# Another order of the parts of an attention step, and other last steps, in a fused attention and MoE kernel on one Trainium2 core

## The chip, the core and the metric

The kernel runs on one core of a Trainium2 chip. The core has a matrix engine (TensorE, PE in the rows; its weight loads are shown as PEld), a vector engine (DVE), an activation engine (ACT), GpSimd (POOL) and a sync engine (SP), which here issues all transfers. Each works through its own list of instructions in the order in which the program was written, and waits where an operand or a buffer is not ready. The metric is the time of one execution in microseconds, lower is better.

## What is computed

Causal attention over 2 batches of 12 heads (sequence 448, head size 64), then two blocks of matrix products over the 896 tokens, all in float32:

```python
scores = scale * np.matmul(q, k.transpose(0, 1, 3, 2))
scores = np.where(mask, -1000000000.0, scores)
scores = scores - np.max(scores, axis=-1, keepdims=True)
attn = np.exp(scores)
attn = attn / (np.sum(attn, axis=-1, keepdims=True) + 1e-09)
x = (attn @ v), heads side by side          # 896 x 768
h = np.maximum(np.maximum(x @ w1, x @ w2), x @ w3)      # 768 x 768 each
x = h @ w_out                                           # 768 x 768
h = x @ w_in                                            # 768 x 2048
r = np.maximum(h, 0.0)
out = (s * (r * r) + b) @ w_out2                        # 2048 x 768
```

## The kernel before

**Attention.** Two heads make a pair; 12 pairs are worked through in steps. `emit(p)` (line 434) writes the instructions of step p, for p from -1 to 13, by walking through one list of names, `ORDER` (line 28). One step holds parts of three pairs, and the list alone decides where each instruction stands on its engine. The names:

- `Sa` (of pair p+1), `Sb`, `Sc` (of pair p): scores on PE, of query tiles 1 and 0, of tile 2, of tile 3 (of 4 tiles of 112 rows). Each fills a PSUM tile `s`, of which there are two, so `Sb` needs the tile that `Sc` of the step before filled, `Sc` that of `Sa`, and the next `Sa` that of `Sb`.
- `Ra`, `Rb`, `Rc`: row maxima on DVE. `Ea`, `Eb`, `Ec`: exponentials on ACT, which read `s` and so set it free. (`Ra` belongs to the `Sa` that stands in the same step, `Ea` reads it in the next.)
- `TA0 TA1 TA2 TB0 TB1 TB2`: 20 transposes of the exponentials of pair p-1 on PE (A and B are the two heads) into three PSUM tiles `t`; `VA0` to `VB2`: their copies to SBUF (tile `PT`) on ACT.
- `N1 N2`: the row sums, 1e-9 added and inverted, on DVE. `RT`: their transpose on PE, which is written into the tile of `TB1`. `RV`: copy on DVE, `Q1`: store to DRAM on SP; one step later `Q2` reads it back spread over the partitions (tile `rb`).
- `PV`: the 16 products with v of pair p-2 on PE. `XM`: divided (times `rb`) on DVE, `XO` and `XL`: split into a high and a low part of x on POOL.
- `LD`: loads on SP of pair p+3; `QS`, `HS`, `LS`: scaling (POOL), high part (DVE) and low part (POOL) of q and k of pair p+2.

**Weights.** Each weight tile (128 x 768, 8-byte words, 768 KB) comes by `fetch_w` and is taken apart in two halves, "chunks", by `decode` (line 137): two passes on ACT, three on DVE (`second` and `third` are put off to `finish`, name `Y` in the list), one addition on POOL (`rounded`, one chunk later), a copy of the high part on ACT, a subtraction of the low part on DVE (`split`, two chunks later). `W1`, `W2`, `W3` each begin a chunk; `CHUNKS` says in which steps. The third weight tile can only be fetched once the second chunk has been read, since there are two raw tiles.

**Early products.** Two of the products of the first MoE block need only batch 0, whose pairs are done half way through. `early_products` (line 521) is a generator over 12 pieces of three matmuls, and `M` in the list (`EARLY`, line 36) takes six of them in step 12 and six in step 13. The product of the first weight tile leaves PSUM by a copy on ACT that stands at the head of the generator's second half.

**MoE.** `moe()` then runs 1404 and 672 matmuls back to back on PE, with one chunk per product.

Of the kernel before, what the change touches and what calls it, by code (L numbers as in the profile page):

```python
# [8 lines left out]
F32 = mybir.dt.float32  # L9
# [6 lines left out]
ALU = mybir.AluOpType  # L16
# [7 lines left out]

ORDER = (
    "Q2 LD TA0 TA1 TA2 Ea N1 N2 Sb Rb VA0 VA1 VA2 Y W1 Sc Eb Rc Y QS PV XM HS XO LS XL "
    "TB0 VB0 TB1 VB1 RT RV Q1 Y W2 TB2 VB2 M Y Sa Y W3 Ra Ec Y"  # L30
).split()


FETCH = 9
CHUNKS = {10: "W3", 11: "W2", 12: "W1 W2 W3", 13: "W1 W2"}
EARLY = {12: 6, 13: 6}
MASKED = -(2.0 ** 30)
OVER = 122880.0
UNDER = 2.0 ** -15
# [9 lines left out]
def kernel(  # L49
# [36 lines left out]
    ident = const.tile([128, 128], F32, name="ident")  # L86
    sb = const.tile([128, 2], F32, name="sb")
    ones = const.tile([128, 512], mybir.dt.bfloat16, name="ones")

    def sub_lo(eng, lo, full, hi):  # L90
        eng.tensor_tensor(out=lo, in0=full, in1=hi.bitcast(F32), op=ALU.subtract)  # L91
# [45 lines left out]
    def decode():  # L137
        if not raws:
            return
        c = n_chunk[0] % 2  # L140
        mine = []
        n_chunk[0] += 1
        raw = raws.pop(0) if c else raws[0]
        words = raw.bitcast(I32).rearrange("p (n t) -> p n t", t=2)
        cs = slice(c * HW, (c + 1) * HW)
        a = wa_p.tile([128, HW], I32, tag="wa", name="wa")
        r = wd_p.tile([128, HW], I32, tag="wr", name="wr")
        f = a.bitcast(F32)
        low, high = (words[:, cs, n] for n in range(2))
        fhigh = raw.bitcast(F32).rearrange("p (n t) -> p n t", t=2)[:, cs, 1]  # L150
        nc.scalar.activation(out=r, in_=low.bitcast(U32), func=ACTF.Copy, scale=2.0 ** -29)  # L151
        nc.scalar.activation(out=f, in_=fhigh, func=ACTF.Abs)  # L152
        nc.vector.tensor_scalar(  # L153
            out=f, in0=f, scalar1=UNDER, scalar2=OVER, op0=ALU.max, op1=ALU.min
        )

        def second():
            nc.vector.tensor_scalar(  # L158
                out=a, in0=a, scalar1=3, scalar2=0x3FFFFFF8,
                op0=ALU.logical_shift_left, op1=ALU.bitwise_and,  # L160
            )

        def third():
            nc.vector.scalar_tensor_tensor(  # L164
                out=a, in0=high, scalar=-0x40000000, in1=a,
                op0=ALU.bitwise_and, op1=ALU.bitwise_or,
            )
            if c:
                fetch_w()

        def rounded():
            nc.gpsimd.tensor_tensor(out=a, in0=a, in1=r, op=ALU.add)  # L172
            if c == 0:
                tiles["w"] = (
                    w_p.tile([128, DM], F32R, tag="whi", name="whi"),
                    w_p.tile([128, DM], F32R, tag="wlo", name="wlo"),
                )
            mine.extend(tiles["w"])
            hi = mine[0]
            rest.append(lambda: nc.scalar.copy(out=hi[:, cs], in_=f))  # L180

        def split():
            hi, lo = mine
            sub_lo(nc.vector, lo[:, cs], f, hi[:, cs])
            if c:
# [14 lines left out]
    def attention():  # L200
        with ExitStack() as c2:
# [104 lines left out]

                return maxima, exponentials

            def pool_copy(out, in_):
                nc.gpsimd.tensor_scalar(  # L310
                    out=out, in0=in_, scalar1=1.0, scalar2=1.0, op0=ALU.mult, op1=ALU.mult
                )

            def weights_out(p, ps):

                e = pair[p]
# [55 lines left out]

            def pv_out(p):
                b, kx = p // NP, p % NP
                e = pair[p]
                x = n_p.tile([128, S], F32, tag="xf", name="xf")
                hi, lo = (xt[kx][:, n, b * S:(b + 1) * S] for n in range(2))

                def divide():
                    nc.vector.tensor_tensor(  # L380
                        out=x, in0=e["o"][:, 0:S], in1=e["rb"], op=ALU.mult
                    )

                def high():
                    pool_copy(hi, x)

                def low():
                    sub_lo(nc.gpsimd, lo, x, hi)

                return divide, high, low  # L390

# [42 lines left out]
            def emit(p):  # L434
# [18 lines left out]
                if 0 <= p - 1 < n_pairs:  # L453
                    d = {}
                    for h, k in enumerate("AB"):
                        for n, js in (("0", (0,)), ("1", (1,)), ("2", (2, 3))):
                            ops["T" + k + n] = lambda n=k + n, h=h, js=js: d.update(
                                {n: transpose_p(p - 1, h, js)}
                            )
                            ops["V" + k + n] = lambda n=k + n: nc.scalar.copy(  # L460
                                out=d[n][0], in_=d[n][1]
                            )
                    su = pair[p - 1]["su"]
# [11 lines left out]
                    ops["Q1"] = lambda: pair[p - 1]["r"][2]()  # L475
                if 0 <= p - 2 < n_pairs:
                    ops["Q2"] = lambda: pair[p - 2]["r"][3]()
                    ops["PV"] = lambda: pv(p - 2, (0, 1, 2, 3))
                    for n, fn in zip(("XM", "XO", "XL"), pv_out(p - 2)):
                        ops[n] = fn  # L480
                if p in EARLY:
                    ops["M"] = lambda: [next(first, None) for _ in range(EARLY[p])]
# [3 lines left out]
                for n in ORDER:  # L486
# [10 lines left out]
            for _ in first:  # L497
                pass


    t_p = ctx.enter_context(tc.tile_pool(name="tmp", bufs=4))
    early = {}
# [18 lines left out]
    def early_products(pool, tag):  # L521
# [164 lines left out]
```

## Time and profile before

| | |
|---|---|
| time, median of 3 runs | 551.66 us (549.05 to 557.89) |
| time of the profiled execution | 549.17 us |
| its span, first to last instruction | 547.4 us |
| busy: PE, PEld, DVE, ACT, POOL | 94%, 84%, 61%, 56%, 43% |
| first MoE matmul of the unbroken stream | at 142.46 us |

Busy shares are means over a kernel of two different halves: up to 142 us attention, then a stream of matmuls. Times in the rows are microseconds from the span's start. A matmul's end is modelled, so where one group of matmuls stops is better read from the start of the next instruction on PE.

### The profile page before, as it was taken

The page shows a single profiled execution, that of the slowest core. Times are in us where ns is not written, and L with a number is a line of the kernel's source. Part 1 is how long each engine was busy: PE and PEld are TensorE (multiplying, and loading weights), DVE is VectorE, ACT ScalarE, POOL GpSimd, SP SyncE. Part 2 cuts the span into 40 slices and gives each one's busy share as a digit, 9 for nine tenths or more (in the row PEclk, how much of TensorE's full clock was granted, in tenths as well). Part 3 has the DMA queues.
Part 4 walks back from the last instruction along what each step waited for, and adds up shares of the span by engine and source line. Part 5 has one row for each costly group of instructions (what it writes and reads, how often), then busy time and mean ns, then how long its engine had stood idle before and what let it go on. Part 6 is the DMA issues. An engine that isn't in the chain of part 4 may idle for free.

```text
span 547.4 us, 8432 instructions
## 1 busy us (share of the span) xinstructions
PE 517.3 (94%) x3094; PEld 461.0 (84%) x3094; DVE 331.7 (61%) x637; ACT 308.6 (56%) x743; POOL 233.0 (43%) x218
## 2 busy tenths in 40 slices
PE   8988878876999999999999999999999999999997
PEld 4656565645899999999999999999999999999997
DVE  3456565547565756566566666676778875567601
ACT  3577776765344534535455478888888743344301
POOL 4336364324343534434433346655665633324200
PEclk9999999978899999999999999999999999999999
DMA  7042422422333223333232233333222353253102
GB/s 235 18 136 74 130 83 72 147 79 76 116 105 127 73 101 122 110 117 117 106 115 90 102 108 117 115 116 115 92 90 109 115 173 112 89 187 121 57 1 101
DMA packets 16185, 58.39 MB, mean 107 GB/s; under 512 B 2384, under 2 KB 6224, under 8 KB 16144
## 3 DMA queue, kind: packets, MB, share of 16 engines
q1 hardware_dynamic: 16144, 57.85, 32.0%
q8 instruction: 24, 0.39, 0.3%
q14 instruction: 17, 0.14, 0.1%
HBM read 55.05 MB, written 2.80 MB: 106 GB/s over the span
## 4 chain that ended last, share of the span: by engine, by line
PE 89%; ACT 6%; DVE 2%; DMA 1%; POOL 1%; issue 1%; ACTq 0%; DVEq 0%; POOLq 0%
PE m L510 53%; PE m L619 21%; PE o L365 4%; PE s L277 4%; ACT P L301 3%; PE t L350 2%; ACT PT L460 2%; PE warm L423 2%; DVE mx L293 2%; DMA wraw<-in_w_dram 1%; PE s L284 1%; PE warm L395 1%; PE t L323 1%; POOL wa L172 0%; ACT wr L151 0%
## 5 line engine op out<-in xcount | busy, mean ns | idle before, releaser
L510 PE MATMUL m<-x,whi 128*128 128x448 f32 x816 | 234.0, 368 | 4.6 <-ACT t L519 3.8
L172 POOL TENSOR_TENSOR wa<-wa,wr 128x384 int32<-128x384 int32 x112 | 129.3, 1154 | 215.7 <-DVE wa L164 185.1
L510 PEld LDWEIGHTS m<-x,whi 128*128 128x128 f32 x816 | 154.6, 190 | 17.5 <-ACT t L519 4.0
L510 PE MATMUL m<-x,wlo 128*128 128x448 f32 x408 | 150.1, 368 | 0.0
L153 DVE TENSOR_SCALAR wa<-wa 128x384 f32<-128x384 f32 x112 | 71.1, 635 | 82.4 <-ACT wa L152 82.4
L619 PE MATMUL m<-whi,g 128*128 128x384 f32 x448 | 113.8, 334 | 0.0
L180 ACT CAST whi<-wa 128x384 fp32r<-128x384 f32 x112 | 56.9, 509 | 79.0 <-PE m L619 36.7
L510 PEld LDWEIGHTS m<-x,wlo 128*128 128x128 f32 x408 | 77.4, 190 | 6.2
L619 PEld LDWEIGHTS m<-whi,g 128*128 128x128 f32 x448 | 81.0, 188 | 0.0
L91 DVE TENSOR_TENSOR wlo<-wa,whi 128x384 fp32r<-128x384 f32 x112 | 62.6, 560 | 23.5 <-ACT whi L180 23.5
L619 PE MATMUL m<-wlo,g 128*128 128x384 f32 x224 | 74.8, 334 | 0.0
L164 DVE SCALAR_TENSOR_TENSOR wa<-wraw,wa 128x384 int32<-128x384 int32 x112 | 62.8, 560 | 3.9
L151 ACT ACTIVATE wr<-wraw 128x384 int32<-128x384 uint32 x112 | 61.4, 549 | 0.2 <-DMA wraw<-in_w_dram 0.2
L152 ACT ACTIVATE wa<-wraw 128x384 f32<-128x384 f32 x112 | 60.6, 541 | 0.0
L301 ACT ACTIVATE P<-s,mx 112x224 f32<-112x224 f32 (+3 forms) x96 | 46.8, 502 | 14.1 <-DVE mx L293 13.7
L293 DVE TENSOR_REDUCE mx<-s 112x2 f32<-112x448 f32 (+3 forms) x48 | 34.0, 731 | 27.4 <-PE s L284 27.3
L158 DVE TENSOR_SCALAR wa<-wa 128x384 int32<-128x384 int32 x112 | 42.8, 382 | 3.8
L460 ACT COPY PT<-t 112x336 f32<-112x336 f32 (+1 forms) x72 | 30.6, 484 | 25.2 <-PE t L350 25.0
L619 PEld LDWEIGHTS m<-wlo,g 128*128 128x128 f32 x224 | 42.0, 188 | 0.0
L510 PE MATMUL m<-h,whi 128*128 128x448 f32 x144 | 40.9, 365 | 0.0
L277 PE MATMUL s<-HL 64*112 64x224 f32 (+3 forms) x288 | 31.3, 331 | 8.3 <-ACT P L301 8.3
L91 POOL TENSOR_TENSOR g<-r,g 128x448 fp32r<-128x448 f32 x32 | 37.2, 1163 | 0.0
(55 smaller groups left out, 485.5 us busy)
## 6 DMA issues: line engine op xcount, KB each, us to landing
wraw<-in_w_dram SPq DMA_DIRECT2D x56, 768.0 KB
R<-in_qk_dram SPq DMA_DIRECT2D x11, 448.0 KB
V<-in_v_dram SPq DMA_DIRECT2D x12, 224.0 KB
rb<-rcd SPq DMA_DIRECT2D x24, 112.0 KB
out_dram<-o SPq DMA_DIRECT2D x14, 192.0 KB
R<-in_qk_dram SPq DMA_DIRECT2D x2, 224.0 KB
rcd<-rows SPq DMA_DIRECT2D x12, 3.5 KB
sb<-in_s_dram SPq DMA_DIRECT2D x1, 0.5 KB
```

The lines of the kernel that those rows point to most:

```text
L91: eng.tensor_tensor(out=lo, in0=full, in1=hi.bitcast(F32), op=ALU.subtract)
L151: nc.scalar.activation(out=r, in_=low.bitcast(U32), func=ACTF.Copy, scale=2.0 ** -29)
L152: nc.scalar.activation(out=f, in_=fhigh, func=ACTF.Abs)
L153: nc.vector.tensor_scalar(out=f, in0=f, scalar1=UNDER, scalar2=OVER, op0=ALU.max, op1=ALU.min)
L164: nc.vector.scalar_tensor_tensor(out=a, in0=high, scalar=-0x40000000, in1=a, op0=ALU.bitwise_and, op1=ALU.bitwise_or,)
L172: nc.gpsimd.tensor_tensor(out=a, in0=a, in1=r, op=ALU.add)
L180: rest.append(lambda: nc.scalar.copy(out=hi[:, cs], in_=f))
L277: nc.tensor.matmul(ps[:, h, o:o + n], hl[h][:, a, qs], hl[h][:, c, 0:n], start=(m == 0), stop=False, skip_group_check=True,)
L293: nc.vector.tensor_reduce(out=e["mx"][:, i], in_=ps[:, :, o:o + n], op=ALU.max, axis=mybir.AxisListType.X, negate=True,)
L301: nc.scalar.activation(out=e["P"][:, h, poff[i]:poff[i] + n], in_=ps[:, h, o:o + n], func=ACTF.Exp, bias=e["mx"][:, i, h:h + 1], scale=1.0 ...
L510: nc.tensor.matmul(p, wt[w][:, ws], cols(act[i], a, b), start=(i == 0 and n == 0), stop=(i == len(act) - 1 and n == 2),)
L619: nc.tensor.matmul(acc[t][:, 0:EH], gt[f][:, a, ts], w[:, ws], start=(f == 0 and n == 0), stop=(f == KG - 1 and n == 2),)
```

## The change

- `ORDER` is replaced: within a step the scores `Sc` and `Sa` now come after all 20 transposes, the product with v is last on PE (split in four names `P0` to `P3`, of two to six instructions that are the same as before), and `RT` stands ahead of the copies `VB0`, `VB1` instead of behind them.
- Steps 12 and 13 have lists of their own, `ORDER_END`. Step 13 holds the product with v of the last pair, then both early products, `M1` and `M2`, each with the copy (or maximum) that takes it out of PSUM right behind its matmuls.
- Chunks: one in step 10, one in step 11, two in step 12, three in step 13 (before one, one, three, two). They start at another place of the step.
- The first two chunks are "light": the absolute value is taken on DVE (`bitwise_and`) instead of ACT, and the high part of the first of them is copied on POOL instead of ACT.
- Step 12 takes `VA1` and `VB1` on DVE. The last two pairs take the high part of x on ACT, the last also its low part on DVE. The last pair's product with v goes to an `s` tile, so that it need not wait for the only `o` tile.

```diff
-EARLY = {12: 6, 13: 6}
-CHUNKS = {10: "W3", 11: "W2", 12: "W1 W2 W3", 13: "W1 W2"}
+CHUNKS = {10: "W1", 11: "W1", 12: "W1 W2", 13: "W1 W2 W3"}
+LIGHT = 2
...
-    "Q2 LD TA0 TA1 TA2 Ea N1 N2 Sb Rb VA0 VA1 VA2 Y W1 Sc Eb Rc Y QS PV XM HS XO LS XL "
+    "TA0 Q2 LD Ea TA1 QS VA0 Sb TA2 VA1 VA2 Rb N1 N2 W1 HS TB0 TB1 RT Eb RV Q1 Y TB2 Sc Sa "
+    "P0 Rc VB0 VB1 Ra Y VB2 P1 P2 P3 LS XM XO XL Ec"
...
+    "P0 P1 P2 P3 Q2 W1 M1 Y Y W2 XM XO XL M2 Y Y W3 Y Y".split(),
...
-        nc.scalar.activation(out=f, in_=fhigh, func=ACTF.Abs)
+        light = n_chunk[0] <= LIGHT
+        if light:
+            nc.vector.tensor_scalar(
+                out=a, in0=high, scalar1=0x7FFFFFFF, scalar2=None, op0=ALU.bitwise_and
+            )
+        else:
+            nc.scalar.activation(out=f, in_=fhigh, func=ACTF.Abs)
...
-            rest.append(lambda: nc.scalar.copy(out=hi[:, cs], in_=f))
+            if light and c == 0:
+                pool_copy(hi[:, cs], f)
+            else:
+                rest.append(lambda: nc.scalar.copy(out=hi[:, cs], in_=f))
...
-                    e["o"] = ps_o.tile([128, 512], F32, tag="o", name="o")
+                    if p == n_pairs - 1:
+                        e["o"] = ps_s.tile([128, 2, 512], F32, tag="s", name="o")[:, 0]
+                    else:
+                        e["o"] = ps_o.tile([128, 512], F32, tag="o", name="o")
...
             for i in range(KD):
                 terms(p[:, m], early["w"][m], xt, 0, i)
-                yield
             evacuate_max(p[:, m], early["t"], m)
+            yield
```

On PE, one step in the middle of attention (s are scores, with the causal mask added by further rows that are left out; t transposes; o the product with v; the lone `t<-ident,su` is `RT`). Before:

```order
L350 MATMUL t<-ident,P 112x112 x10
L277 MATMUL s<-HL 112x336 x6
...
L277 MATMUL s<-HL 112x448 x6
...
L365 MATMUL o<-PT,V 64x448 x2
...
L350 MATMUL t<-ident,P 112x112 x7
L323 MATMUL t<-ident,su 8x112
L350 MATMUL t<-ident,P 112x112 x3
L277 MATMUL s<-HL 112x224 x6
```

and with the change:

```order
L364 MATMUL t<-ident,P 112x112 x7
L296 MATMUL s<-HL 112x336 x6
...
L364 MATMUL t<-ident,P 112x112 x10
L337 MATMUL t<-ident,su 8x112
L364 MATMUL t<-ident,P 112x112 x3
L296 MATMUL s<-HL 112x448 x6
...
L296 MATMUL s<-HL 112x224 x6
...
L382 MATMUL o<-PT,V 64x448 x2
```

The product with v moved from the middle of the step, between the scores of tile 3 and the second head's transposes, to its end, behind the next pair's first scores.

On DVE, the same step (mx are the maxima, `su` the row sums `N1` and `N2`, xf is `XM`, HL is `HS`, rows is `RV`). Before, from `Ra` on, and with the change, from `Rb` on:

```order
L293 TENSOR_REDUCE mx<-s 112x2 x2
L464 TENSOR_SCALAR su<-su 112x8
L467 RECIPROCAL su<-su 112x8
L293 TENSOR_REDUCE mx<-s 112x2 x2
L380 TENSOR_TENSOR xf<-o,rb 128x448
L239 CAST HL<-R 128x2x448
L326 COPY rows<-t 8x112
```

```order
L312 TENSOR_REDUCE mx<-s 112x2
L487 TENSOR_SCALAR su<-su 112x8
L490 RECIPROCAL su<-su 112x8
L258 CAST HL<-R 128x2x448
L340 COPY rows<-t 8x112
L312 TENSOR_REDUCE mx<-s 112x2 x3
L397 TENSOR_TENSOR xf<-o,rb 128x448
```

The two row-sum instructions now stand behind `Rb`, and `XM` is the last of a step, ahead of the next step's `Rb`.

On ACT, the end of attention up to the copy that takes the first early product out of PSUM (wr and wa are the two passes of a chunk over its raw tile, whi its high part). Before, and with the change:

```order
L151 ACTIVATE wr<-wraw 128x384
L152 ACTIVATE wa<-wraw 128x384
L180 CAST whi<-wa 128x384
L151 ACTIVATE wr<-wraw 128x384
L152 ACTIVATE wa<-wraw 128x384
L519 COPY t<-m 128x448
```

```order
L161 ACTIVATE wr<-wraw 128x384
L168 ACTIVATE wa<-wraw 128x384
L199 CAST whi<-wa 128x384
L161 ACTIVATE wr<-wraw 128x384
L168 ACTIVATE wa<-wraw 128x384
L540 COPY t<-m 128x448
```

The rows read alike. The last chunk ahead of the copy is the fifth in both, the first half of the third weight tile; what moved is the matmuls: before, PE has 16 products with v of the last pair between the two early products, with the change both early products follow each other.

## Rows read from the trace of the kernel before

**Rows 1.** Stretches: busy us (instructions) of PE, PEld, DVE, ACT, POOL; PEclk, DMA share, GB/s.
```profile
40.00:60.00 20.00, 16.14 (x173) 11.74 (x169) 11.53 (x20) 13.58 (x47) 9.84 (x9) 1.00 0.29 97
119.00:121.00 2.00, 2.00 (x7) 0.77 (x8) 0.40 (x2) 1.81 (x5) 0.00 (x0) 0.50 0.95 381
```
**Rows 2.** Waits of PE from 25 to 104 us: us in total, times, longest.
```profile
PE s L277 <- ACT P L301: 8.3, 9, 0.9
PE t L323 <- ACT PT L460: 6.1, 9, 0.7
```
**Rows 3.** Timeline of one step: start us, us, engine, line, operation, tiles, count [idle before].
```profile
60.01 0.26 PE L323 MATMUL t<-ident,su 112*8 112x112 f32 x1 [0.68 <-ACT PT L460]
...
60.49 0.56 PE L277 MATMUL s<-HL 64*112 64x224 f32 x6
...
61.48 1.17 PE L350 MATMUL t<-ident,P 112*112 112x112 f32 x10
...
61.59 0.92 DVE L293 TENSOR_REDUCE mx<-s 112x2 f32<-112x448 f32 x2 [1.02 <-PE s L284]
...
62.15 1.14 POOL L91 TENSOR_TENSOR x<-xf,x 128x448 fp32r<-128x448 f32 x1
62.43 0.89 DVE L464 TENSOR_SCALAR su<-su 112x8 f32<-112x8 f32 x1
...
62.58 0.72 PE L277 MATMUL s<-HL 64*112 64x336 f32 x6
...
63.26 0.56 POOL L233 TENSOR_SCALAR R<-R 128x448 f32<-128x448 f32 x1
...
63.47 0.83 DVE L293 TENSOR_REDUCE mx<-s 112x2 f32<-112x672 f32 x1
...
64.32 0.86 PE L277 MATMUL s<-HL 64*112 64x448 f32 x6 [0.92 <-ACT P L301]
...
65.22 2.11 PE L365 MATMUL o<-PT,V 112*64 112x448 f32 x16
...
65.33 1.09 DVE L293 TENSOR_REDUCE mx<-s 112x2 f32<-112x896 f32 x1 [1.03 <-PE s L284]
...
67.25 0.88 PE L350 MATMUL t<-ident,P 112*112 112x112 f32 x7
67.37 0.62 DVE L380 TENSOR_TENSOR xf<-o,rb 128x448 f32<-128x448 f32 x1 [0.95 <-PE o L365]
```
**Rows 4.** Timeline: the first transposes of step 2 and of step 11.
```profile
26.26 1.17 PE L350 MATMUL t<-ident,P 112*112 112x112 f32 x10
...
105.49 0.50 PE L350 MATMUL t<-ident,P 112*112 112x112 f32 x3
```
**Rows 5.** Chain that ended last: start us, us, what (62 us: one step; then the end).
```profile
62.63 1.65 ACT P L301 x8
...
67.89 0.88 ACT PT L460 x2
...
135.05 6.64 PE m L510 x18
...
142.46 284.81 PE m L510 x1404
```
**Rows 6.** Waits of PE from 104 to 143 us.
```profile
PE m L510 <- ACT t L519: 3.8, 1, 3.8
PE t L350 <- ACT P L301: 3.2, 2, 2.6
```
**Rows 7.** Timeline: fetches of weight tiles, and the divisions whose rb stood behind them.
```profile
96.12 1.17 SPq L134 DMA_DIRECT2D wraw<-in_w_dram  x2
...
105.19 0.62 DVE L380 TENSOR_TENSOR xf<-o,rb 128x448 f32<-128x448 f32 x1 [3.56 <-PE s L284]
...
129.09 0.36 SPq L134 DMA_DIRECT2D wraw<-in_w_dram  x1
...
134.52 0.62 DVE L380 TENSOR_TENSOR xf<-o,rb 128x448 f32<-128x448 f32 x1 [1.43 <-DMA rb<-rcd]
```

More of the change, by code (lines that the diff above doesn't have):

```diff
@@ L28 @@
 ORDER = (
-    "Q2 LD TA0 TA1 TA2 Ea N1 N2 Sb Rb VA0 VA1 VA2 Y W1 Sc Eb Rc Y QS PV XM HS XO LS XL "
-    "TB0 VB0 TB1 VB1 RT RV Q1 Y W2 TB2 VB2 M Y Sa Y W3 Ra Ec Y"
+    "TA0 Q2 LD Ea TA1 QS VA0 Sb TA2 VA1 VA2 Rb N1 N2 W1 HS TB0 TB1 RT Eb RV Q1 Y TB2 Sc Sa "
+    "P0 Rc VB0 VB1 Ra Y VB2 P1 P2 P3 LS XM XO XL Ec"
 ).split()
+ORDER_END = (
+    "TA0 VA0 TA1 VA1 TA2 VA2 Q2 N1 N2 TB0 VB0 TB1 RT VB1 RV Q1 TB2 VB2 W1 P0 P1 P2 P3 Y Y "
+    "XM XO XL W2 Y Y".split(),
+    "P0 P1 P2 P3 Q2 W1 M1 Y Y W2 XM XO XL M2 Y Y W3 Y Y".split(),
+)
 FETCH = 9
-CHUNKS = {10: "W3", 11: "W2", 12: "W1 W2 W3", 13: "W1 W2"}
-EARLY = {12: 6, 13: 6}
+CHUNKS = {10: "W1", 11: "W1", 12: "W1 W2", 13: "W1 W2 W3"}
+LIGHT = 2
 MASKED = -(2.0 ** 30)
@@ L88, with pool_copy @@
     ones = const.tile([128, 512], mybir.dt.bfloat16, name="ones")
+    def pool_copy(out, in_):
+        nc.gpsimd.tensor_scalar(
+            out=out, in0=in_, scalar1=1.0, scalar2=1.0, op0=ALU.mult, op1=ALU.mult
+        )
     def sub_lo(eng, lo, full, hi):
@@ L151, in decode @@
         nc.scalar.activation(out=r, in_=low.bitcast(U32), func=ACTF.Copy, scale=2.0 ** -29)
-        nc.scalar.activation(out=f, in_=fhigh, func=ACTF.Abs)
+        light = n_chunk[0] <= LIGHT
+        if light:
+            nc.vector.tensor_scalar(
+                out=a, in0=high, scalar1=0x7FFFFFFF, scalar2=None, op0=ALU.bitwise_and
+            )
+        else:
+            nc.scalar.activation(out=f, in_=fhigh, func=ACTF.Abs)
         nc.vector.tensor_scalar(
@@ L307, in scores @@
                 return maxima, exponentials
[L309 to L312, printed above, removed]
             def weights_out(p, ps):
@@ L384, in high @@
                 def high():
-                    pool_copy(hi, x)
+                    if p < n_pairs - 2:
+                        pool_copy(hi, x)
+                    else:
+                        nc.scalar.copy(out=hi, in_=x)
                 def low():
-                    sub_lo(nc.gpsimd, lo, x, hi)
+                    sub_lo(nc.gpsimd if p < n_pairs - 1 else nc.vector, lo, x, hi)
                 return divide, high, low
@@ L459, in emit @@
                             )
-                            ops["V" + k + n] = lambda n=k + n: nc.scalar.copy(
+                            copy = nc.scalar.copy
+                            if p == n_pairs and n == "1":
+                                copy = nc.vector.tensor_copy
+                            ops["V" + k + n] = lambda n=k + n, copy=copy: copy(
                                 out=d[n][0], in_=d[n][1]
@@ L477, in emit @@
                     ops["Q2"] = lambda: pair[p - 2]["r"][3]()
-                    ops["PV"] = lambda: pv(p - 2, (0, 1, 2, 3))
+                    for j in range(NC):
+                        ops[f"P{j}"] = lambda j=j: pv(p - 2, (j,))
                     for n, fn in zip(("XM", "XO", "XL"), pv_out(p - 2)):
                         ops[n] = fn
-                if p in EARLY:
-                    ops["M"] = lambda: [next(first, None) for _ in range(EARLY[p])]
+                if p == n_pairs + 1:
+                    ops["M1"] = ops["M2"] = lambda: next(first)
                 for n in CHUNKS.get(p, "").split():
@@ L485, in emit @@
                 ops["Y"] = lambda: finish(1)
-                for n in ORDER:
+                for n in ORDER if p < n_pairs else ORDER_END[p - n_pairs]:
                     if n in ops:
@@ L496, in attention @@
                     fetch_w()
-            for _ in first:
-                pass
     t_p = ctx.enter_context(tc.tile_pool(name="tmp", bufs=4))
```

## The prediction

> **What bounds the kernel now.** I first read the stretches, for where PE is not the bound. From 142.46 us on PE runs 1404 matmuls in 284.81 us without a gap, 0.203 us each [rows 5]; the change touches nothing there but the first chunks, so what can be won lies ahead of 142.46. In the middle of attention PE is busy 16.14 of 20 us, ACT 13.58, DVE 11.53, POOL 9.84 [rows 1]: no engine is full, so it is the order that costs. The waits say which: nine times PE waits some 0.92 us before scores, for exponentials, and nine times some 0.68 us before the row-sum transpose, for a copy [rows 2]. Nine steps, from step 2's first transposes to step 11's, take 105.49 - 26.26 = 79.23 us, 8.80 each [rows 4].
>
> The timeline of one step gives PE's work, from the start of one group to that of the next [rows 3]: `RT` with three transposes 0.48 (60.01 to 60.49); `Sa` 0.99 (to 61.48); ten transposes 1.10 (to 62.58), so 0.11 each; `Sb` 0.82 (64.32 less the wait of 0.92, less 62.58); `Sc` 0.90 (64.32 to 65.22); the product with v 2.03 (to 67.25); seven transposes 0.77 at 0.11. That is 7.09 of work, 1.60 of waits, and 0.11 left over. Why `Sc` waits: it takes the PSUM tile of `Sa`, which is last in a step, so maxima (0.92) and exponentials (1.65 in all) [rows 3, 5] have only ten transposes and `Sb` to hide under. Why `RT` waits: it writes into the tile that `VB1` still copies.
>
> **The steady step, part by part.** `Sa` now precedes the product with v, so its maxima and exponentials have 2.03 us more cover, and `Sc` comes after all transposes: the 0.92 goes. `RT` stands ahead of `VB1`: the 0.68 goes. Matmuls and their sizes are the same. What is late next? `RT` needs the inverted sums, `N1` and `N2`, and these now stand behind `Rb` on DVE. I walk one step from its first transposes at 0. `TA0`, `TA1` take 0.77, `Sb` ends at 1.59, `Rb` starts 0.11 later (as 61.59 follows 61.48) and ends at 2.53 with its 0.83 [rows 3]. On PE three and seven transposes reach 2.69. On POOL: the product with v ended at 0, `XM` starts 0.12 after it (67.37 to 67.25) and takes 0.62, to 0.74; `XO` some 0.56 by the like `QS`, to 1.4 with its start; `XL` 1.14, to 2.6. In the row of before `N1`, 8 elements wide, lasts 0.89, and it ends at 63.32, just as `XL` does (62.15 + 1.14 = 63.29) [rows 3]: it is held by POOL. So here it ends at about 2.64, `N2` fits in 0.15 (63.32 to 63.47), and `RT` starts at 2.85: a wait of 0.16. Then 0.48, 0.90, 0.99 and 2.03 to 7.25.
>
> The Trainium skill, page "SBUF — State Buffer", section "Who interferes with whom", says that DVE and GpSimd share one port pair, as a lock that whoever issues first holds for its whole instruction. The trace agrees with the lock (0.89 us for `N1`).
>
> The rest fits in 7.25: `Rc` from 4.34 to 5.43, `Ra` behind it to 6.4, `Ec` after `Rc` at most 1.65, to 7.1, before `Sb` of the next step at 8.0; `Ea` from 7.1 to 8.8, two copies at 0.44 [rows 5] to 9.7, which is 2.4 into the next step, where `TB1` needs the second from 2.3 on: even with this upper bound, 0.1. `HS` waits for `QS` until about 3.2, `RV` and `VB1` are behind it, and nothing on PE needs them before the next step. `rb` is asked for at the start of a step and read at its end. With the same 0.11 over, a step is 7.09 + 0.16 + 0.11 = **7.36**, 1.44 less than 8.80; nine give **13.0**. Step 1 has the wait for `VB1` too, so some **0.7** more; its warm-up matmuls stay.
>
> **Chunks in steps 10 and 11.** Two raw tiles are fetched behind step 9's `Q1`, some 4.5 us into that step. Before, tiles and `rb` of 96.12 were in at 105.19 at the latest [rows 7], 9.1 later; here that is 6.2 us into step 10, and `XM`, now last, asks at 7.4. So the late `XM` of step 10 goes, without time of its own. The light chunk moves a pass from ACT to DVE. Nothing of before shows this `bitwise_and`; I bound it by `N2`'s 0.15 and, behind a POOL instruction, by `XL`'s 1.14, and take 0.5, nearest to `XM`, a DVE pass over 448 columns in 0.62 where this one has 384. In step 10 three such passes and `RV` meet a gap of 1.5 us between `N2` and `Rc`; `Rc` is 0.3 late at most, and `Ec` still ends with the product with v. In step 11 POOL's addition and copy of chunk 1 stand beside chunk 2, and I let `Rc` and so `Ec` come 0.6 late.
>
> **The end**, from step 11's first transposes: 36.97 us before (142.46 - 105.49). Now step 11 has no `Sa`: 7.36 - 0.99 = 6.4. Step 12 has 20 transposes and `RT`, 2.3 of work; `Ec` is 0.6 late, and the wait for copies and for `N1` behind `XL` I set at 0.7, between nothing and the 2.6 that such a wait for exponentials lasted before [rows 6]: to 10.0. A stretch of transposes with holes is where the clock fell before: behind the wait of 2.6, from 119 to 121, the granted clock was 0.50 [rows 1], the 1.2 GHz level, and after a wait of 3.8 us the 18 matmuls from 135.05 took 6.64 instead of 18 x 0.203 = 3.65, 1.82 times as long [rows 5, 6]. I let one product with v run so: 3.7, to 13.7. The other 2.0, to 15.7. First early product 3.65, to 19.4; its copy out of PSUM 0.8 (as 141.69 to 142.46 before [rows 5]), to 20.2; second 3.65, to 23.8; 0.8 again, **24.6**. That is 36.97 - 24.6 = **12.4** less.
>
> What must hide under it: `XM` of pair 10 needs `rb` behind the third weight tile, which is fetched at about 6.7 (after chunk 2's last pass) and was in 134.52 - 129.09 = 5.4 later with `rb` [rows 7]: 12.1, against 13.7. ACT reaches the third tile at about 16 and finds it there; before, PE stood 3.8 us for the copy behind it [rows 6]. Taking copies to DVE and x's high part to ACT at the end costs nothing as long as that holds; else each is one 0.44 or 0.62 on the path.
>
> **Sum.** 0.7 + 13.0 + 12.4 = 26.1, off the profiled execution's 549.17 (its span 547.4, and 1.8 around it): **523.1 us**. That execution is 2.5 below the median of the runs shown and next to their lowest, so I take it as the typical one and leave 2.5 of room above.
>
> **Rivals.**
> - *POOL holds `N1` longer.* `QS` follows `XL` on POOL without a gap; if it is taken first, `N1` ends 0.56 later [rows 3]. For it: `N1` waits right at that seam. Against: in the row `N1` was out at 63.32 though `QS` stood ready at 63.26. Nine times 0.56: 528.1. By the Trainium skill's rule that whoever issues first holds the lock, this is what an earlier `QS` would do.
> - *The clock holds at the end.* Waits in step 12 are short. 1.7 less: 521.4.
> - *A weight comes late in steps 12 and 13*: the chain of ACT, DVE and POOL per chunk outlasts the matmuls. As long as the wait of before, 3.8 [rows 6]: 526.9.
> - *The steps don't get shorter*: `XM`, now ahead of the next `Rb` on DVE, waits for `rb`, `Rb` and `RT` follow. It needs `rb` 1.44 us behind the product with v in each step. Against: `rb` is asked for a step earlier, and only fetches of 768 KB held it. Then only the end is won: 536.8.
> - *Slower*: the clock falls in the steady steps, where PE now does transposes and scores for 5 us before the product with v. At 1.82 times, 7.09 becomes 12.9, 5.8 more per step; the forecast's gain is gone from the fifth such step on (26.1 / 5.8 = 4.5), nine give 575. Against: from 40 to 60 the clock was 1.00 with longer waits than are left [rows 1].
>
> **Chances.** Forecast 0.51 (519 to 527 by itself), held `N1` 0.14, clock holds 0.13, late weight 0.13, steps as long 0.05, clock falls 0.04. The range reaches from the case without clock loss and without the wait of 0.16 (some 518) to held `N1` with 2.5 of spread above, 531. Within 2% of 551.66, 540.6 to 562.7, is about what a measurement of this kernel can't tell from no change; only a few slow-clock steps end there or above: faster 0.94, same 0.03, slower 0.03.
>
> **What would show it.** First transposes of neighbouring steps 7.2 to 7.5 us apart; no wait of PE for exponentials before `Sc`, none for a copy before `RT`, but a short one for DVE's reciprocal; `N1` ending with `XL`. The first unbroken MoE matmul at 116 us. A step of 7.9 means that `QS` holds `N1`; 8.8 that the step is bound elsewhere; a granted clock of 0.50 outside step 12, or a wait of over 2 us in the early products, makes the end wrong.

## The result, and the profile after

The changed kernel takes 523.73 us (median of 4 runs, 523.55 to 526.89) against 550.66 us before (4 runs, 549.05 to 557.89): a ratio of 0.953, 95% interval 0.948 to 0.959. The profiled execution took 523.55 us, its span is 521.6 us, against 549.17 and 547.4. The forecast was 523.1 with a range of 518 to 531. The total is right; two of its terms are not, in opposite directions.

In the changed kernel line numbers are 10 to 23 higher: L364 is a transpose of exponentials, L337 the transpose of the sums (`RT`), L296 and L303 scores, L382 the product with v, L312 maxima, L320 exponentials, L483 their copies, L487 and L490 `N1` and `N2`, L397 `XM`, L96 and L101 the copy (`XO`) and the subtraction (`XL`) that split x, L405 the same copy on ACT, L531 a product of the first MoE block, L540 and L538 the copy and the maximum that take it out of PSUM. I read three pieces in it, as in the prediction: from the start of the program to the first transposes of step 2 (the head), nine steps from there to step 11's, and the end, from there to the unbroken stream.

**The steps.** Waits of PE in the changed kernel from 24 to 91 us (us in total, times, longest), which answer to [rows 2]:

```profile
PE t L337 <- DVE su L490: 1.7, 8, 0.2
PE t L364 <- ACT PT L483: 1.2, 1, 1.2
```

The two waits that came nine times before, 0.9 for exponentials and 0.7 for a copy, are gone. What is left is the announced short wait for the reciprocal, and one wait of 1.2 us that nobody announced. One step in the timeline of the changed kernel (start, us, engine, line, operation, tiles, count [idle before]), against [rows 3]:

```profile
57.90 0.89 PE L364 MATMUL t<-ident,P 112*112 112x112 f32 x7
...
58.02 0.62 DVE L397 TENSOR_TENSOR xf<-o,rb 128x448 f32<-128x448 f32 x1 [0.98 <-PE o L382]
...
59.38 1.14 POOL L101 TENSOR_TENSOR x<-xf,x 128x448 fp32r<-128x448 f32 x1
...
59.46 1.17 PE L364 MATMUL t<-ident,P 112*112 112x112 f32 x10
59.58 0.86 DVE L312 TENSOR_REDUCE mx<-s 112x2 f32<-112x672 f32 x1 [0.94 <-PE s L303]
60.35 0.19 DVE L487 TENSOR_SCALAR su<-su 112x8 f32<-112x8 f32 x1
...
60.58 0.20 DVE L490 RECIPROCAL su<-su 112x8 f32<-112x8 f32 x1
...
60.84 0.26 PE L337 MATMUL t<-ident,su 112*8 112x112 f32 x1 [0.20 <-DVE su L490]
...
61.32 0.86 PE L296 MATMUL s<-HL 64*112 64x448 f32 x6
...
62.09 0.55 PE L296 MATMUL s<-HL 64*112 64x224 f32 x6
...
63.07 2.11 PE L382 MATMUL o<-PT,V 112*64 112x448 f32 x16
...
65.11 0.88 PE L364 MATMUL t<-ident,P 112*112 112x112 f32 x7
```

`Sc` (61.32), `Sa` (62.09) and the product with v (63.07) follow each other without a gap, and a step lasts 65.11 - 57.90 = 7.21 us, against 8.80. PE is busy 19.58 of 20 us in this stretch, against 16.14 [rows 1]:

```profile
40.00:60.00 20.00, 19.58 (x223) 14.69 (x220) 12.26 (x25) 17.39 (x61) 11.96 (x11) 1.00 0.39 116
...
103.00:107.00 4.00, 4.00 (x33) 2.20 (x33) 3.29 (x8) 2.28 (x6) 0.97 (x2) 1.00 0.43 144
```

**The end.** The second of these stretches (columns as in [rows 1]) is that of the last two products with v, at a granted clock of 1.00, the 2.4 GHz level; before, a stretch at this place had 0.50 [rows 1]. The timeline of the end:

```profile
93.98 0.88 PE L364 MATMUL t<-ident,P 112*112 112x112 f32 x7
...
100.33 1.18 PE L364 MATMUL t<-ident,P 112*112 112x112 f32 x10
101.67 0.88 PE L364 MATMUL t<-ident,P 112*112 112x112 f32 x7 [0.15 <-ACT PT L483]
...
102.87 4.00 PE L382 MATMUL o<-PT,V 112*64 112x448 f32 x32
106.79 0.67 PE L531 MATMUL m<-x,whi 128*128 128x448 f32 x2
...
111.38 0.67 PE L531 MATMUL m<-x,whi 128*128 128x448 f32 x2 [0.67 <-ACT t L540]
...
115.53 0.63 DVE L101 TENSOR_TENSOR x<-xf,x 128x448 fp32r<-128x448 f32 x1 [0.63 <-ACT x L405]
...
116.07 0.61 DVE L538 TENSOR_TENSOR t<-t,m 128x448 f32<-128x448 f32 x1
...
116.73 0.67 PE L531 MATMUL m<-x,whi 128*128 128x448 f32 x2 [1.45 <-DVE t L538]
```

Step 12 begins at 100.33, both products with v fill 102.87 to 106.79, the first block of early products runs to the wait ahead of 111.38, the second to that ahead of 116.73. From there the chain of the changed kernel has the same stream as [rows 5], moved forward by 25.73 us:

```profile
116.73 284.81 PE m L531 x1404
```

**The head.** First the start of the kernel before, then of the changed one (timeline of PE; L395, L423, L415 and L443 are warm-up products on a tile of ones, L277 and L296 the first scores):

```profile
1.45 3.58 PE L395 MATMUL warm<-ones 128*128 128x512 bf16 x9 [1.45 <-DVE ones L401]
5.75 2.12 PE L423 MATMUL warm<-ones 128*128 128x512 bf16 x9 [0.72 <-DVE ones L405]
7.79 0.57 PE L277 MATMUL s<-HL 64*112 64x224 f32 x6
```

```profile
1.45 4.02 PE L415 MATMUL warm<-ones 128*128 128x512 bf16 x9 [1.45 <-DVE ones L421]
6.19 4.02 PE L443 MATMUL warm<-ones 128*128 128x512 bf16 x9 [0.72 <-DVE ones L425]
10.14 0.83 PE L296 MATMUL s<-HL 64*112 64x224 f32 x6
```

The first nine products take 4.02 us instead of 3.58 and the second nine 4.02 instead of 2.12, so the first scores start 2.35 us later. The trace shows a granted clock of 1.00 in these stretches in both kernels; that the products run at the lower level while they take twice as long is read from their lengths alone. The edit touches nothing up to there. The experiments come back to it.

### The profile page after: what moved, and what is told of

Same layout as the page of the kernel before. It is cut to its first block, busy times and chain, and to the rows that moved or that the text cites. A ratio compares the mean times of both kernels' runs of the same rounds, so it can differ in the third digit from the quotient of the medians.

```text
span 521.6 us, 8414 instructions
## 1 busy us (share of the span) xinstructions
PE 510.2 (98%) x3091; PEld 456.2 (87%) x3094; DVE 328.5 (63%) x642; ACT 307.4 (59%) x740; POOL 229.8 (44%) x216
## 4 chain that ended last, share of the span: by engine, by line
PE 92%; DVE 4%; ACT 1%; DMA 1%; issue 1%; POOL 0%; SPq 0%; ACTq 0%; DVEq 0%
PE m L531 55%; PE m L640 22%; PE s L296 5%; PE o L382 4%; PE warm L443 2%; PE t L364 2%; DVE mx L312 2%; PE s L303 1%; DMA rb<-rcd 1%; PE warm L415 1%; ACT P L320 0%; PE t L337 0%; DVE wa L169 0%; DVE su L490 0%; POOL x L101 0%
## 5 line engine op out<-in xcount | busy, mean ns | idle before, releaser
L531 PE MATMUL m<-x,whi 128*128 128x448 f32 x816 | 232.0, 366 | 2.1 <-DVE t L538 1.4
L531 PEld LDWEIGHTS m<-x,whi 128*128 128x128 f32 x816 | 153.0, 188 | 15.0 <-DVE t L538 1.8
L531 PE MATMUL m<-x,wlo 128*128 128x448 f32 x408 | 149.0, 365 | 0.0
L531 PEld LDWEIGHTS m<-x,wlo 128*128 128x128 f32 x408 | 76.6, 188 | 6.1
L101 DVE TENSOR_TENSOR wlo<-wa,whi 128x384 fp32r<-128x384 f32 x112 | 62.3, 557 | 21.6 <-ACT whi L199 21.6
L320 ACT ACTIVATE P<-s,mx 112x224 f32<-112x224 f32 (+3 forms) x96 | 46.3, 496 | 19.1 <-DVE mx L312 18.9
L312 DVE TENSOR_REDUCE mx<-s 112x2 f32<-112x448 f32 (+3 forms) x48 | 33.6, 737 | 25.5 <-PE s L303 25.5
L531 PE MATMUL m<-h,whi 128*128 128x448 f32 x144 | 40.9, 365 | 0.0
L101 POOL TENSOR_TENSOR g<-r,g 128x448 fp32r<-128x448 f32 x32 | 37.2, 1163 | 0.0
L101 POOL TENSOR_TENSOR HL<-R,HL 128x896 fp32r<-128x896 f32 x11 | 23.0, 2093 | 21.9 <-DVE HL L258 21.9
L364 PE MATMUL t<-ident,P 112*112 112x112 f32 x240 | 30.2, 264 | 1.4 <-ACT PT L483 1.4
```

The source lines that it names most:

```text
L312: nc.vector.tensor_reduce(out=e["mx"][:, i], in_=ps[:, :, o:o + n], op=ALU.max, axis=mybir.AxisListType.X, negate=True,)
L320: nc.scalar.activation(out=e["P"][:, h, poff[i]:poff[i] + n], in_=ps[:, h, o:o + n], func=ACTF.Exp, bias=e["mx"][:, i, h:h + 1], scale=1.0 ...
L531: nc.tensor.matmul(p, wt[w][:, ws], cols(act[i], a, b), start=(i == 0 and n == 0), stop=(i == len(act) - 1 and n == 2),)
```

## The experiments

All kernels side by side, each piece from the profiled execution, the medians from all runs. Pieces are the safer reading: in one profile below the whole MoE stream ran 2% slower than in the others, and two of the four times of another are 5 to 7 us above the other two. The times of e2 and e3, whose intervals reach up to 1.001 and 0.997, would settle little by themselves. The kernel before had medians of 549.0, 549.8 and 549.7 us beside the three groups of experiments.

| kernel | first scores | step 2 begins | nine steps | end | stream begins | median, us | ratio (95%) |
|---|---|---|---|---|---|---|---|
| before | 7.79 | 26.26 | 79.23 | 36.97 | 142.46 | 550.66 | 1 |
| changed | 10.14 | 28.00 | 65.98 | 22.75 | 116.73 | 523.73 | 0.953 (0.948 to 0.959) |
| e1 new order, old end | 10.04 | 27.64 | 66.30 | 30.28 | 124.22 | 530.77 | 0.966 (0.960 to 0.972) |
| e2 old order, new end | 10.14 | 28.84 | 79.22 | 29.36 | 137.42 | 545.65 | 0.990 (0.978 to 1.001) |
| e3 old, only `RT` early | 7.96 | 25.60 | 71.73 | 36.24 | 133.57 | 542.65 | 0.988 (0.979 to 0.997) |
| e4 changed, `RT` late | 10.10 | 28.54 | 72.42 | 23.39 | 124.35 | 529.08 | 0.963 (0.958 to 0.969) |
| e5 changed, `N1 N2` first | 8.13 | 25.72 | 63.19 | 22.78 | 111.69 | 518.37 | 0.944 (0.938 to 0.950) |
| e6 changed, no light chunks | 8.24 | 25.86 | 66.25 | 22.68 | 114.79 | 521.35 | 0.947 (0.941 to 0.954) |
| e7 changed, last `XL` later | 7.67 | 25.28 | 65.93 | 22.24 | 113.45 | 522.84 | 0.952 (0.946 to 0.957) |
| e8 changed, v ahead of `Sa` | 10.14 | 27.80 | 75.49 | 24.06 | 127.35 | 534.00 | 0.973 (0.967 to 0.979) |
| e9 changed, one fill | 8.24 | 25.83 | 65.95 | 22.99 | 114.77 | 521.10 | 0.948 (0.944 to 0.952) |
| e10 e5, e7 and e9 | 7.34 | 24.93 | 63.17 | 21.89 | 109.99 | 519.51 | 0.943 (0.936 to 0.951) |
| e11 e10, fewer warm-ups | 7.88 | 23.94 | 63.64 | 21.64 | 109.22 | 516.12 | 0.937 (0.932 to 0.942) |

### The two halves of the change, one at a time

e1 is the kernel before with the new order up to step 11 and the old order of names and old code behind it (its chunks of steps 10 and 11 begin where the new order has `W1`); e2 the reverse.

```diff
 e1:
+ORDER = ( ...the new one... )
-for n in ORDER:
+for n in ORDER if p < n_pairs else ORDER_END:     # ORDER_END: the old list
 e2:
 ORDER = ( ...the old one... )
+the new ORDER_END, CHUNKS from step 12, LIGHT, the copies and M1, M2
```

> The new order of a step alone: steps up to 11 as in the change, but the old list for steps 12 and 13, old early products, no light chunks. Theory (the two halves of the change gain apart from each other, 13 us in the steps and 14 at the end): first transposes of neighbouring steps 7.2 us apart, the end from step 11's first transposes as long as before but for step 11 itself (some 35 to 37 us), time 534 to 538. Rival (the end is set by when the weights come, so that time won in the steps is waited for at the end): the end is longer by what the steps won, time 544 to 549.

> The new end alone: old order of the steps up to 11, new lists for steps 12 and 13, both early products in step 13 with their copies out of PSUM right behind them, light chunks. Theory (halves gain apart): steps 8.80 us apart, from step 11's first transposes to the unbroken stream of the MoE 23 to 26 us instead of 37, no wait of 2 us or more on PE, time 533 to 538. Rival (the end is short only because the new steps begin the weights earlier within steps 10 and 11): a wait of 2 us or more for a weight in the early products, time 539 to 545.

The halves do not divide as I thought. In the nine steps e1 has the changed kernel's time (66.30) and e2 that of before (79.22), as expected. But the end of 36.97 becomes 30.28 by the order alone (-6.7) and 29.36 by the last steps alone (-7.6); together 22.75 (-14.2). The two gains add up, and half of the end belongs to the order of the steady steps. e1's median of 530.77 lies below its forecast of 534 to 538 for this reason. Some 2.8 us of the 6.7 are step 11 itself, which is a step of the new order (6.36 us, against some 9.1 before). Where most of the rest comes from shows in PE's waits from 90 to 145 us, of e1 (there L517 is the early product and L328 `RT`), against [rows 6]:

```profile
PE m L517 <- ACT t L526: 4.6, 1, 4.6
PE t L328 <- ACT PT L465: 1.7, 1, 1.7
```

The wait of 2.6 us for exponentials in step 12 is gone: in the new order they are made under a product with v, one step earlier. With it goes the lower clock behind it. The same 16 products with v, before and then in e1:

```profile
119.10 4.00 PE L365 MATMUL o<-PT,V 112*64 112x448 f32 x16
```

```profile
101.42 2.11 PE L370 MATMUL o<-PT,V 112*64 112x448 f32 x16
```

The wait of before for the copy behind the weight tile is still there (4.6, before 3.8), and behind it the granted clock was 0.57 from 115 to 120 us. In e2 it is the other way round: no wait for that copy above 0.7, but the transposes of step 12 still wait (0.87 for exponentials, 0.73 for a copy), and the last two products with v run in part at the lower clock level (e2, timeline, then stretches, with a granted clock of 0.62):

```profile
121.06 0.35 PE L337 MATMUL t<-ident,su 112*8 112x112 f32 x1 [0.18 <-DVE su L490]
...
121.90 6.36 PE L382 MATMUL o<-PT,V 112*64 112x448 f32 x32
```

```profile
119.00:128.00 9.00, 8.09 (x41) 4.10 (x41) 5.36 (x13) 3.72 (x9) 1.74 (x2) 0.62 0.43 140
```

The same 32 matmuls took 4.00 us in the changed kernel. So the clock held at the end where the order of the steps had closed the gaps ahead of it, and fell where it had not: e2's four runs have a mean granted clock of 0.993 to 0.997, the changed kernel's 0.999 to 1.000. e2's end of 29.36 us misses its forecast of 23 to 26; against the changed kernel these products take 2.4 us more, and steps 11 and 12 ahead of them, with their waits, 4.9 more. Its profile also has the late first scores (10.14) that e1's and the changed kernel's have.

### The early transpose of the sums

e3 is the kernel before with `RT` ahead of `VB1`, e4 the changed kernel with `RT` behind `VB0 VB1`.

```diff
 e3:
-    "TB0 VB0 TB1 VB1 RT RV Q1 Y W2 ...
+    "TB0 VB0 TB1 RT VB1 RV Q1 Y W2 ...
 e4: ORDER of the changed kernel with
-    ... HS TB0 TB1 RT Eb RV ...       P0 Rc VB0 VB1 Ra ...
+    VB0 and VB1 ahead of RT
```

> The kernel before, with one name moved: the row-sum transpose stands ahead of the copy of the second head's second tile. Theory (its wait of 0.68 lies on the cycle of a step): steps 8.1 us apart, ten of them 6.8 less, time 541 to 544. Rival (the wait goes over into the one before the scores of tile 3, which the exponentials end): steps 8.8 apart, time 548 to 550.

> The changed kernel with one part undone: both copies of the second head's tiles stand ahead of the row-sum transpose, which waits for them again. Theory (the place of this transpose is a part of the gain by itself): it starts some 3.55 us into a step instead of 2.94, steps 7.8 apart, time 528 to 530. Rival (with the product with v last, the place of the transpose doesn't matter): steps 7.2 apart, time 523 to 525.

Both times are as the theory had them. e3's steps last 7.97 us (71.73 / 9), where 8.1 was expected: the wait for the copy is gone, that for exponentials stays (7.1 us in eight steps). In e4 steps 3 to 10 start 7.68 us apart, 0.46 more than in the changed kernel, and the 0.7 us wait for the copy is back nine times:

```profile
PE t L337 <- ACT PT L483: 6.1, 9, 0.7
PE t L364 <- ACT PT L483: 1.2, 1, 1.2
```

The early `RT` is worth 0.83 us a step in the old order and 0.46 in the new one, where it runs into the wait for the reciprocal. e4's profile also shows what the slower rival of the prediction looks like when it comes true once: in step 2 the waits of 1.2 and 0.7 us stand 1.6 us apart, behind them the granted clock falls to 0.50, and this step takes 10.6 us (28.54 to 39.16) instead of 8.26:

```profile
34.00:37.00 3.00, 3.00 (x32) 2.60 (x32) 1.09 (x1) 1.06 (x4) 0.12 (x1) 0.50 0.03 7
```

The mean granted clock of e4's four runs was 0.996, 0.996, 0.997 and, in the shortest (527.69 us), 1.000, which suggests that this last one went without it.

### The product with v as cover

```diff
-    ... TB2 Sc Sa P0 Rc VB0 VB1 Ra Y VB2 P1 P2 P3 LS ...
+    ... TB2 Sc P0 P1 P2 P3 Sa Rc VB0 VB1 Ra Y VB2 LS ...
```

> The changed kernel with all four parts of the product with v between Sc and Sa, so that Sa is again the last piece of a step on TensorE. Theory (the product with v earns its gain by lying between Sa and the next step's transposes, where the exponentials and copies of Sa are made): each of nine steps waits 1.0 to 1.2 us for the copies of the exponentials, as step 2 does in the changed kernel, which has no product with v; a step lasts 8.1 to 8.4 us, and the time is 532 to 535. Rival (only the early transpose of the sums and the split of the product matter): steps stay at 7.2, 523 to 525.

The theory holds: 8.39 us a step (75.49 / 9), 534.0 us. Waits of e8's PE from 24 to 91 us:

```profile
PE t L364 <- ACT PT L483: 9.6, 8, 1.2
```

It is the wait of 1.2 us that the changed kernel has once, in step 2. Step 1 has no product with v (there is no pair for it yet), so step 2's exponentials (of the `Sa` at 27.00) end at about 30.7 and the copies, which stand behind them on ACT, come late. That explains why step 2 takes 8.26 us and the other eight 7.215 (57.72 / 8).

### What the reciprocal waits for

```diff
-    "TA0 Q2 LD Ea TA1 QS VA0 Sb TA2 VA1 VA2 Rb N1 N2 W1 HS ...
+    "TA0 Q2 LD Ea TA1 QS VA0 Sb TA2 VA1 VA2 N1 N2 Rb W1 HS ...
```

> The changed kernel with N1 and N2 ahead of Rb on VectorE. In the changed kernel the transpose of the sums waits 0.2 us for the reciprocal in each of eight steps (1.7 us in all), and N1 stands behind Rb. Theory 'the order on VectorE decides': N1 (0.16 us by itself) runs at once, ahead of the 0.86 us of Rb, the wait goes, and the time falls by 8 x 0.2 = 1.6 us to 521.9 to 522.4. Theory 'POOL's XL holds N1': XL lies at 59.38 to 60.52 in the step that begins at 57.90, N1 starts beside it and lasts about 1 us until XL ends, the wait of the transpose stays at about 0.2 us, and Rb with the exponentials behind it comes about 1.2 us later: 523.5 to 526.

My rival came from the prediction: POOL's `XL` holds `N1`. The rows of the changed kernel decide against it. In the step shown above `N1` starts 0.77 us after `Rb` (59.58, 60.35) and lasts 0.19, while `XL` runs. In step 2, where POOL has nothing to do for 4.12 us, it starts 0.77 us after `Rb` as well, and lasts 0.16:

```profile
29.68 0.86 DVE L312 TENSOR_REDUCE mx<-s 112x2 f32<-112x672 f32 x1 [0.64 <-PE s L303]
...
30.45 0.16 DVE L487 TENSOR_SCALAR su<-su 112x8 f32<-112x8 f32 x1
...
31.50 2.10 POOL L101 TENSOR_TENSOR HL<-R,HL 128x896 fp32r<-128x896 f32 x1 [4.12 <-DVE HL L258]
```

So `Rb` sets when `N1` starts, and `XL` adds some 0.03 us. e5 by itself would not tell the two apart, since there `N1` stands ahead of `Rb` and runs ahead of `XL` too. One step of e5:

```profile
54.46 0.88 PE L364 MATMUL t<-ident,P 112*112 112x112 f32 x7
54.58 0.63 DVE L397 TENSOR_TENSOR xf<-o,rb 128x448 f32<-128x448 f32 x1 [0.98 <-PE o L382]
...
55.12 0.16 DVE L487 TENSOR_SCALAR su<-su 112x8 f32<-112x8 f32 x1
...
55.29 0.56 POOL L96 TENSOR_SCALAR x<-xf 128x448 fp32r<-128x448 f32 x1 [1.61 <-DVE su L487]
55.31 0.20 DVE L490 RECIPROCAL su<-su 112x8 f32<-112x8 f32 x1
...
56.02 1.17 PE L364 MATMUL t<-ident,P 112*112 112x112 f32 x10
56.13 0.86 DVE L312 TENSOR_REDUCE mx<-s 112x2 f32<-112x672 f32 x1 [0.62 <-PE s L303]
...
57.03 0.26 PE L337 MATMUL t<-ident,su 112*8 112x112 f32 x1
...
61.29 0.88 PE L364 MATMUL t<-ident,P 112*112 112x112 f32 x7
```

`N1` goes right behind `XM`, before POOL's first instruction on the new x begins, and takes 0.16 us. `Rb` waited for its scores in any case, so it is not delayed. No wait of PE is listed any more in steps 3 to 10, and each of steps 3 to 9 lasts 6.83 us; step 10, with the first chunk in it, lasts 7.14, against 7.23 in the changed kernel. 6.83 is 0.385 less than 7.215, though the wait that went was shown with 0.20. The rest is in the overlap of neighbours: here `RT` starts at 57.03, while the ten transposes are modelled to end at 56.02 + 1.17 = 57.19; in the changed kernel they end at 59.46 + 1.17 = 60.63, and `RT` starts 0.21 behind that. The idle column counts from the end, the step from start to start. Nine steps take 2.79 us less (63.19); the other 2.28 us of the lower stream start (111.69 against 116.73, with 0.03 more at the end) are the earlier step 2, 25.72 against 28.00. The median of 518.37 contains both, and so lies below the 521.9 to 522.4 that the theory expected.

### The light chunks and the last `XL`

```diff
 e6:
-LIGHT = 2
+LIGHT = 0
 e7:
-    "P0 P1 P2 P3 Q2 W1 M1 Y Y W2 XM XO XL M2 Y Y W3 Y Y".split(),
+    "P0 P1 P2 P3 Q2 W1 M1 Y Y W2 XM XO M2 XL Y Y W3 Y Y".split(),
```

> The changed kernel with the first two weight chunks done in the old way: the absolute value and the high copy of each back on ScalarE (about 0.55 and 0.5 us there) in place of the clearing of the sign bit on VectorE (0.31 and 1.00 us) and the copy on POOL. In the changed kernel ScalarE has 0.4 to 0.5 us of idle time ahead of the last exponentials of these steps, and TensorE waits for none of its copies there. Theory (light chunks matter little): steps 10 and 11 grow by 0 to 0.6 us each, 523.7 to 524.9 with the first scores at 10.14 (2.0 to 2.4 us less where they start at 7.7 to 8.1). Rival (ScalarE is full there): the copies come 1 us late in both steps, a wait of about 1 us for copies or exponentials shows in each, 525.5 to 526.5.

> The changed kernel with the last XL (the low half of the last x on VectorE, 0.6 us) behind the second block of early products in the order written down, so that it stands behind the maximum of VectorE that the unbroken product stream waits for. Theory: this wait falls from 1.4 to 0.8 us, the stream begins 0.6 us earlier (116.1 instead of 116.7) and the time is 523.1, if the first products that need the late low half come far enough behind. Rival: the stream then waits for that low half, and the time stays at 523.7 or grows by up to 0.6.

e6: nine steps 66.25 against 65.98, the end 22.68 against 22.75; 0.27 more and 0.07 less, so the light chunks are worth some 0.2 us. The median of 521.35 lies below the changed kernel's only by its head (first scores at 8.24). e7: the wait ahead of the unbroken stream is 0.7 instead of 1.4 us, but the one at the second block is 0.9 instead of 0.7, so that the end takes 22.24, 0.5 less, near the forecast. In its profile the stream of 1404 matmuls took 290.42 instead of 284.81 us at a granted clock of 1.00, without a wait; I have no cause for that, and the piece, not the profiled time of 525.78, is what speaks on the edit.

### The start

```diff
             nc.sync.dma_start(out=sb[:, 1:2], in_=b2.to_broadcast([128, 1]))
-            nc.vector.memset(ones, 1.0)
             make_identity(nc, ident)
```

> The changed kernel without the second fill of the warm-up operand (a repetition of the first one, with the same value), for which TensorE waits 0.72 us between its first two blocks of nine warm-up products. In the changed kernel both blocks take 4.02 us (0.45 us a product, the 1.2 GHz level) and the first scores start at 10.14; in the kernel before the level rises inside the first block (3.58 us) and the second takes 2.12, first scores at 7.79. Theory (the pause between the blocks, met before the rise, starts the slow stretch again): without the pause the products run on, the rise comes at about 5 us as in the kernel before, the first scores start at 7.2 to 8.0 and the whole program moves forward by 2 to 2.9 us: 520.8 to 521.7. Rival 1 (the slow stretch is of this program or this run, not of the pause): first scores at 9.0 to 9.4, 522.8 to 523. Rival 2 (the loads and the first splits set the head anyway): first scores come early, the first transposes of step 2 stay at 28.0 and the time at 523.7.

The time is in the theory's range (521.10, runs from 520.93 to 521.71), the first scores (8.24) are a little behind it, and the mechanism is not quite the one I named:

```profile
1.46 4.02 PE L415 MATMUL warm<-ones 128*128 128x512 bf16 x9 [1.46 <-DVE ones L421]
5.27 3.04 PE L442 MATMUL warm<-ones 128*128 128x512 bf16 x9
8.24 0.57 PE L296 MATMUL s<-HL 64*112 64x224 f32 x6
```

By its length all of the first block is at the lower level (4.02 us), and so is about half of the second: 3.04 us lies between 2.12 and 4.02. So the rise does not come at a fixed time: it came inside the first block before, in e3, e5 and e7, in the pause in e6 (4.02, then 2.12), and inside the second block here. Of the ten profiles with the pause, five have first scores at 7.7 to 8.2 us and five at 10.04 to 10.14, nothing between; the changed kernel, e4 and e8 on one side and e5, e6 and e7 on the other have the same code up to there. Of the three without the pause all lie at 7.3 to 8.2. Where the first block took all of 4.0 us, the second took 3.92 to 4.02 in five of six profiles with the pause, and 2.14 to 3.04 in the three without. That fits the pause putting a late rise off, but is not shown by so few; why the rise is early or late in a run stays open.

### The edits that gained, together

e10 is the changed kernel with the edits of e5, e7 and e9; e11 leaves out six warm-up products of step 1 as well.

```diff
-WARM_AT = {(-1, "Sa"): 9, ..., (1, "TA2"): 2, (1, "Sc"): 6}
+WARM_AT = {(-1, "Sa"): 9, ..., (1, "TA2"): 2}
```

> The changed kernel with three edits that each gained alone: N1 and N2 ahead of Rb, the last XL behind the second block of early products, and no second fill of the warm-up operand. If they add up: steps of 6.83 us as with the first edit alone (8 x 0.385 = 3.1 us less), 0.6 us less at the end, 2.2 us less at the start: 523.7 - 5.9 = 517.8, range 517.2 to 518.3. Rival (the start of the first edit's runs was already the early one in most of them, so the third edit adds nothing on the median): 517.6 to 518.4, told from the first by the spread alone (no run 2 us above the median). If they do not add (the earlier start takes away cover): 518.4 to 520.

> The kernel with the three edits, and without the six warm-up products that stand between Sc and Sa in step 1. Step 1 has no product with v, so that in step 2 TensorE waits 1.2 us for ScalarE's copies; Sa of step 2 starts behind these six products (1.3 us). Theory: Sa, its maxima and exponentials start about 1.0 us earlier (limited by POOL's low half of that step, which ends 0.15 us before Sa starts in the changed kernel, or by ScalarE's exponentials ahead of them), the copies come 0 to 0.9 us earlier, and the time is 0 to 0.9 us below that of the kernel with the three edits, nearest 0.2 since POOL's low half ends so late. Rival (TensorE then idles for more than 2 us and the granted clock falls to the lower level in step 2): 0.5 to 2.5 us above it.

In the pieces the three edits add up: nine steps 63.17 (e5 63.19), end 21.89 (changed 22.75), first scores 7.34. The profiled time is 516.91, 1 us below the forecast, since step 2 begins 3.1 us earlier instead of 2.2 and the end gained 0.9 instead of 0.6. The median of 519.51 is of little use here: the four times are 516.4, 516.9, 522.1 and 523.4, and what the longer two lost shows in no profile (5 to 7 us is about what the slow stream cost in e7's). e11's four lie between 515.68 and 516.80: 516.12 us, a ratio of 0.937 to the kernel before and 7.6 us (1.5%) below the changed kernel. The wait of 1.2 us in step 2 falls to two of 0.7, no stretch shows a lower clock, and the stream begins 0.77 us earlier than in e10 (109.22), in the upper part of the 0 to 0.9 expected. But e11's first scores came 0.54 us later than e10's (7.88 and 7.34); counted from them the stream begins 1.31 us earlier, more than expected.

## Why the prediction was right, step by step

- **Two waits a step go: right.** No wait for exponentials ahead of `Sc`, none for a copy ahead of `RT`. e3 and e4 show that the second went by the early `RT`. e8 shows what the product with v covers: without it between `Sa` and the next step, PE waits 1.2 us a step for the copies that stand behind `Sa`'s exponentials. The wait ahead of `Sc` itself did not come back there, since `Sc` still stood behind all transposes; no run tests this place of `Sc` alone.
- **The step of 7.36: close, by two errors that cancel in part.** Eight steps measured 7.215. The work in it was 0.26 too large: e5, where PE waits for nothing, shows 6.83 for what the prediction summed to 7.09, and the 0.11 left over beside it. It had summed rows of a step with waits in it, where each group behind a wait lacks the overlap with its neighbour. And a wait that it put at 0.16 costs 0.385.
- **The wait for the reciprocal: seen, with the wrong cause.** `N1` did end with `XL` (60.54 and 60.52), as announced, but it was hardly held: it lasted 0.19 us, 0.03 longer than with POOL idle, and started when `Rb` ended. `Rb` ahead of it was the cause, and e5 removed it without touching POOL. An announced sign that two causes share decided nothing.
- **Nine equal steps: wrong for the first.** Step 2 took 8.26. The prediction noted that the cover is the product with v, and did not ask in which step there is none. Nine steps, 79.23 - 65.98 = 13.25 less, come to the forecast of 13.0 all the same.
- **The head, 0.7 less: wrong in sum, right in the part it spoke of.** From the first scores to step 2 it was 18.47 us before and is 17.86, 0.6 less. But step 2 begins 1.74 later, because the first scores were 2.35 late, which the prediction had no term for. e5 to e7, with the same code up to there, are without this loss, so it belongs to the execution rather than to the change.
- **The end, 12.4 less: 14.2 measured.** By its steps: step 11 6.35 (6.4 expected), step 12 to its last transposes 2.54 (3.6), the two products with v 3.92 (5.7, for one at half clock), the first block with its wait 4.59 (4.45), the second 5.35 (4.45). The case that the clock holds came true. The prediction had allowed 1.3 for late exponentials and waits in step 12 (0.6 and 0.7), where a wait of 0.15 is left. The second block was longer because the low half of the last x stood ahead of the maximum on DVE, and waited 0.63 us for the high half from ACT (115.53, above). The prediction had put this at nothing as long as no weight came late; e7 took half a microsecond of it back. And the split of the gain was wrong: half of it is the order's (e1, e2).
- **The sum:** +1.74 - 13.25 - 14.22 = -25.7 against the forecast's -26.1. That they agree to 0.4 us is luck: the head came out 2.4 us worse than forecast and the end 1.8 better. In e6 and e9, whose profiles have first scores at 8.24, the times are 521.4 and 521.1, below the forecast and still in its range. None of the other rivals came: no weight was late in the last steps, and the clock stayed at 1.00 in the steady steps, though e4's profile shows it at 0.50 in step 2 behind one more wait near that of 1.2 us.

## What to carry to other kernels

Put the longest piece of independent matrix work between the production of an operand and its use, and then look for the step in which this piece is missing, at the start of the pipeline. When a short wait is left, ask first what stands ahead of the producer on its own engine; moving two small instructions up gave 0.385 us a step, twice what the wait showed. The worth of an edit at the end of a pipeline depends on the gaps left ahead of it, since the same products ran at either clock level (4.00 us in the changed kernel, 6.36 in e2).

## What the runs showed of the hardware

- At the start of the kernel nine warm-up products of 512 columns take 4.02 us or 2.12 us, and the change from one to the other comes at another time in each run, inside the first block, in the pause, or only in or behind the second. This moves the whole program by up to 2.5 us. The traces show a granted clock of 1.00 there all the same.
- A wait of PE costs some 0.2 us more than its idle time shows (0.385 against 0.20 in e5; and 7.68 in e4 is 0.85 above e5's 6.83, for a wait of 0.68), since the modelled end of a group lies about 0.16 us behind the start of a next one that need not wait (57.19 and 57.03 in e5).
